# DCN-v2 cross layers on one core: input loads moved behind output transposes, an output copy two layers later, another order of the first small loads, padded biases

## The chip, the cores and the metric

The kernel runs on one core of a Trainium2 chip. Times are device microseconds of an execution; a kernel's time is the median of several. The profile is of one execution, in which a core's engines are TensorE (PE, with its weight loads as PEld), VectorE (DVE), ScalarE (ACT), GpSimd (POOL) and SyncE (SP). DMA transfers are issued by a queue of SP, of ACT or of POOL and run on 16 DMA engines that all queues share.

## What is computed

Six cross layers on a batch of 4096 rows with 416 features, all in bfloat16:

```python
# x0: (4096, 416), ws: (6, 416, 416), bs: (6, 416)
x = x0
for l in range(6):
    x = x0 * (x @ ws[l] + bs[l]) + x
return x
```

## The kernel before

**Algebra.** Every layer adds x0 times something to x. So x after layer l is x0 times (1 + the sum of all products and biases so far), and the kernel lets the matmuls of all layers add up in PSUM: a layer's output is (sum + cb[l]) * x0, where cb[l] is 1 plus the biases of layers 0 to l. These sums are made once, on PE, as a product of the biases (with a row of ones) and a triangle `u_sb` (`bias_sums`, B_BANK is bank 6), and evicted by ACT into `cb_sb`.

**Tiling.** Features lie on partitions, batch rows on the free axis. The batch is cut into four superblocks of 1024 rows (`s`, SB = 1024), each in two halves `h` of 512. The 416 features are three chunks of 128 (`c`, `m`, `k`) and a tail of 32. The tail of the four quarters of a superblock is packed onto 128 partitions (`x0t_sb`, `xt_sb`), beside a copy with neighbouring quarters exchanged ("swapped"). Six PSUM banks hold the sums of chunk m and half h, two more the tail's. Matmuls use 32-column strips of the array for the chunks, and 32-row strips for the tail inputs.

**A layer**, for each superblock: nine groups of main matmuls for half 0 (`main`), then the tail's contribution to all outputs (`tail_rows`, which needs the tail weights `wt_sb` and their corner `wc_sb`), then DVE makes half 0's next input (`leave`, L426), the tail's outputs (`tail_outs`), the tail's own eviction on ACT, its product on POOL (L449) and the swaps, split over ACT (L413) and POOL (L415), and the main matmuls and `leave` of half 1. In the last superblock's last layer, batch rows are put on partitions instead, and DVE, ACT and POOL multiply with rows of x0 (`xr_sb`) and store.

**Order of the work.** The program of each engine is written out by `Plan` in the order of the calls; every engine works through its own list in order and waits on semaphores that `Plan` derives from what is read and written. So where a call stands in the text decides what it waits behind on its engine.

**The head.** Fourteen matmuls on a constant (`fill`, L288) keep PE occupied. Superblock 0's first half is loaded as rows (`load_rows`: xin0 by SP, xin1 by ACT), transposed on PE (L497) and copied by DVE (L506); its second half, and the later superblocks, are transposed by DMA (`load_transposed`, L205, on SP). Of the tail, superblock 0's is transposed on PE from the rows and from `xtl_sb` (the tail columns of rows 512 to 1023, 128 x 4 x 32 elements), in `tail_in`, and evicted by ACT (L402). ACT's queue has, in this order: xin1, xtl, the biases `bsa_sb` (L234), and layer 0's tail weights wt0 in four pieces (L235). On PE, layer 0 goes: main k = 0, `bias_sums`, main k = 1, `tail_in`, main k = 2, `tail_rows`.

**Later superblocks.** Before, SP issues all input loads at the start: weights, then for superblocks 1, 2, 3 the transposed chunks and the last columns (`load_last_columns`, L211), then `xr_sb` (L244 to L249). `place_tail` (L219, six DMAs) puts a superblock's tail into its packed form; superblock 1's is in that list, the next ones' are issued in layer 2 of the superblock before. At a superblock's end, `transpose_block` issues four DMA transposes: three of the outputs `xo_sb` (L466) and one of the tail's `xot_sb` (L471). `store_block` (POOL's copy L477 of the tail's output, then the store L483 on SP) follows in layer 1 of the next superblock, behind that layer's tail product and swaps and ahead of the next layer's on POOL (L566, L567).

Of the kernel before, what the change touches and what calls it, by code (L numbers as in the profile page):

```python
# [118 lines left out]
def bass_standalone__dcn_v2_cross__recsys_kernel(  # L119
# [6 lines left out]
    B, D = x0.shape  # L126
    L = ws.shape[0]
# [4 lines left out]
    SB = 1024  # L132
    NS = B // SB
    H = SB // 2
    G = SB // 4
    JS = SB // 128
    NJ = B // 128
# [4 lines left out]
    with ExitStack() as es:  # L142

        def sb(name, shape, dt=BF16):
            return es.enter_context(nc.sbuf_tensor(name, shape, dt))
# [7 lines left out]
        xr_sb = sb("xr_sb", [128, JS, D])  # L153
        x0T_sb = sb("x0T_sb", [128, NC, B])
# [11 lines left out]
        ident = sb("ident", [128, 128])  # L166
        ones_sb = sb("ones_sb", [128, 128])
        dummy_sb = sb("dummy_sb", [128, 8])
        bsa_sb = sb("bsa_sb", [L + 1, D])
        u_sb = sb("u_sb", [L + 1, L])  # L170
        cb_sb = sb("cb_sb", [128, NC + 1, L], FP32)
        bt_sb = sb("bt_sb", [128, 1], FP32)
        ps = es.enter_context(nc.psum_tensor("ps", [128, 8, 512], FP32))
# [14 lines left out]
        def load(queue, dst, src, name, writes):  # L188
            P.add(queue, lambda e: e.dma_start(dst, src), writes=writes, dma=name)  # L189
# [9 lines left out]
        def load_tail_weights(a, b, name, queue="sync"):  # L199
            for q in range(4):  # L200
                load(queue, wt_sb[quad(q), a:b, :], ws[a:b, DF:D, :].rearrange("l p n -> p l n"), name, [("wt", name)])

        def load_transposed(s, a, b):
            P.add(
                "sync", lambda e: e.dma_start_transpose(x0T_sb[:, :, s * SB + a:s * SB + b], x0[s * SB + a:s * SB + b, 0:DF]),  # L205
                writes=[("x0T", s, c, h) for c in CH for h in HALVES if a <= h * H < b], dma="x0T%d" % s,
            )

        def load_last_columns(s):
            P.add(  # L210
                "sync", lambda e: e.dma_start_transpose(tT_sb[:, s - 1, :], x0[s * SB:(s + 1) * SB, D - 128:D]),  # L211
                writes=[("tT", s)], dma="tT%d" % s,
            )

        def place_tail(s):
            def part(g, o, n):
                dst, src = x0t_sb[quad(g), s, o:o + n, :], tT_sb[128 - DR:128, s - 1, (g ^ o) * G:((g ^ o) + n) * G]
                P.add(
                    "sync", lambda e: e.dma_start(dst, src.rearrange("p (o c) -> p o c", o=n)), reads=[("tT", s)],  # L219
                    writes=[("x0t", s), ("x0t", s, "swapped")], dma="x0t%d" % s,  # L220
                )

            for g in (0, 2):
                part(g, 0, 2)
            for g in (1, 3):
                part(g, 0, 1)
                part(g, 1, 1)
# [2 lines left out]
        load_rows("scalar", 1)  # L230
        for k in CH:
            load("sync", w_sb[:, 0, k, :], ws[0, 128 * k:128 * k + 128, :], "w0_%d" % k, [("w", 0, k)])
        load("scalar", xtl_sb[:, 4:JS, :], x0_v[:, 4:JS, DF:D], "xtl0", [("xtl", 0)])
        load("scalar", bsa_sb[1:L + 1, :], bs[:, :], "bs", [("bs",)])  # L234
        load_tail_weights(0, 1, "wt0", "scalar")  # L235
        load_transposed(0, H, SB)
        load_main(1)
        load_tail_weights(1, 2, "wt1")
# [2 lines left out]
        load_main(3)  # L241
        load_main(4)
        load_main(5)
        for s in range(1, NS):  # L244
            load_transposed(s, 0, SB)
            load_last_columns(s)
            if s == 1:
                place_tail(1)
        load("sync", xr_sb[:, :, :], x0_v[:, (NS - 1) * JS:NJ, :], "xr", [("xr",)])  # L249


        P.add("vector", lambda e: e.memset(ones_sb[:, :], 1.0), writes=[("ones",)])
# [7 lines left out]
                compare_op=ALU.is_equal, fill=0.0, base=0, channel_multiplier=1,  # L260
            ), reads=[("ones",)], writes=[("ident",)],
        )
        P.add("gpsimd", lambda e: e.memset(bsa_sb[0:1, :], 1.0), writes=[("bs1",)])
        P.add(
            "gpsimd", lambda e: e.affine_select(
                out=u_sb[:, :], in_=ones_sb[0:L + 1, 0:L], pattern=[[1, L]],
                compare_op=ALU.is_ge, fill=0.0, base=1, channel_multiplier=-1,
            ), reads=[("ones",)], writes=[("u",)],
        )
# [221 lines left out]
        for i in range(2):  # L491
            for c in CH:
                b = HEAD_BANKS[i][c]

                def fn(pe, i=i, c=c, b=b):
                    for j in range(2):
                        ins = pe.transpose(  # L497
                            out=psT[:, b, j * 128:(j + 1) * 128],
                            in_=xin_sb[:, 2 * i + j, c * 128:(c + 1) * 128], identity=ident[:, :],
                        )  # L500
                    return ins

                P.add("tensor", fn, reads=[("xin", i), ("ident",)], adds=[("ps", b)])
                dst, src = x0T_sb[:, c, i * 256:(i + 1) * 256], psT[:, b, 0:256]
                P.add(
                    "vector", lambda e, d=dst, s=src: e.tensor_copy(out=d, in_=s),  # L506
                    reads=[("ps", b)], writes=[("x0Tp", c, i)],
                )
        for c in CH:
            P.writer[("x0T", 0, c, 0)] = [w for i in range(2) for w in P.writer[("x0Tp", c, i)]]  # L510

        def bias_sums():
            def fn(pe):
                for c in range(NC + 1):
                    for q in range(4):
                        f0 = c * 128 + (32 * q if c < NC else 0)
                        ins = mm(
                            pe, ps[quad(q), B_BANK, c * 8:c * 8 + L], bsa_sb[:, f0:f0 + 32], u_sb[:, :],
                            c == 0, (0, 32 * q),
                        )  # L520
                return ins

            P.add("tensor", fn, reads=[("bs",), ("bs1",), ("u",)], adds=[("ps", B_BANK)])
            P.add(
                "scalar", lambda e: e.activation(
                    out=cb_sb[:, :, :],
                    in_=ps[:, B_BANK, 0:8 * (NC + 1)].rearrange("p (c e) -> p c e", e=8)[:, :, 0:L], func=ACTF.Copy,
                ), reads=[("ps", B_BANK)], writes=[("cb",)],
            )
# [3 lines left out]
        for s in range(NS):  # L533
            for l in range(L):
                ending = s == NS - 1 and l == L - 2
                if s == NS - 1 and l == L - 1:
                    break
                if s == 0 and l == 0:
                    for k in CH:
                        for part in range(2) if k == 0 else (None,):  # L540
                            for m in CH:
                                main(s, l, 0, m, k, part)
                        if k == 0:
                            bias_sums()
                        if k == 1:
                            tail_in()
                    tail_rows(s, l, True)
                    for c in CH:
                        leave(s, l, 0, c)
                    tail_outs(s, l, False)  # L550
                else:
                    for m in CH:
                        for k in CH:
                            main(s, l, 0, m, k)
                    tail_rows(s, l, l == 0)
                    for c in CH:
                        leave(s, l, 0, c)
                    tail_outs(s, l, False)
                if s == 0 and l == 1:
                    corner(2, L, "wt2")  # L560
                leave_tail(s, l, not ending)
                if l == 2 and 0 < s < NS - 1:
                    place_tail(s + 1)
                if s == 0 and l == 0:
                    corner(1, 2, "wt1")
                if l == 1 and s > 0:  # L566
                    store_block(s - 1)  # L567
                if ending:
                    P.add(
                        "gpsimd", lambda e: e.tensor_tensor(  # L570
                            out=bt_sb[:, :], in0=cb_sb[:, NC, L - 1:L], in1=cb_sb[:, NC, L - 2:L - 1], op=ALU.subtract
                        ), reads=[("cb",)], writes=[("bt",)],
                    )
                    P.add(
                        "gpsimd", lambda e, t=t32_sb[:, l % 2, :]: e.tensor_scalar_add(st_sb[:, :], t, bt_sb[:, :]),
                        reads=[("t32", l % 2), ("bt",)], writes=[("st",)],
                    )
                    for c in CH:
                        keep_sum(0, c, "scalar")
                for m in CH:  # L580
                    for k in CH:
                        main(s, l, 1, m, k)
                    leave(s, l, 1, m)
                if ending:
                    for c in CH:
                        keep_sum(1, c, ("scalar", "scalar", "vector")[c])
            if s < NS - 1:
                transpose_block(s)


        s, l = NS - 1, L - 1
# [128 lines left out]
```

## Time and profile before

| what | value |
| --- | --- |
| time, median of 3 runs | 129.0 us (128.87 to 129.28) |
| profiled execution, its own time | 130.0 us |
| its span, first to last instruction | 128.5 us |
| granted TensorE clock | 1.00 |
| L426, DVE's product into xT_sb, 120 of them | 80.9 us, 743 ns each |
| L280, PE's matmuls from xT_sb, 1596 of them | 84.2 us, 364 ns each (they overlap) |
| DMA queue of SP (q1) | 33744 packets, 13.20 MB, 48.5% of 16 engines |
| DMA queue of ACT (q10) | 1292 packets, 0.57 MB, 1.7% |

The page's busy times say which engine is nearly always at work; the chain names the work that ended last, followed back from the end; the waits say who stood still for whom, as a total, a count and the longest. In the timeline, each line has a start and a length in microseconds from the span's start, the engine (a q marks its queue of DMA issues), the line of code, the operation, and in brackets the idle time before it with what ended it. The prediction shows the lines that it rests on.

### The profile page before, as it was taken

To read this page: it belongs to the slowest core of one execution; us is meant where nothing else is said; L and a number is where in the kernel's file an instruction comes from. 1 tells how busy PE (TensorE), PEld (TensorE's weight loads), DVE (VectorE), ACT (ScalarE), POOL (GpSimd) and SP (SyncE) were. 2 spreads that over 40 slices of the span, in tenths; PEclk is the share of its full clock that TensorE was granted. 3 is DMA by queue.
4 is the path that set the end of the run, shared out by engine and by line. 5 is a ranking of instruction groups with operands and counts; after the bars stand their busy time and mean duration, and the time that the engine had idled before them with its cause. 6 is when DMAs were issued, how large, how long until landed. Compare 5 with 4: busy or idle time off the path is not lost.

```text
span 128.5 us, 5300 instructions
## 1 busy us (share of the span) xinstructions
PE 123.2 (96%) x2414; PEld 64.3 (50%) x2414; DVE 98.5 (77%) x152; ACT 43.5 (34%) x95; POOL 37.4 (29%) x79
## 2 busy tenths in 40 slices
PE   7979999999999999799999999999999999999991
PEld 5544554555545545345545545545555455455660
DVE  0329779779779779497797797797797797797973
ACT  0515225225205222343222252252222252253920
POOL 6005224134014040442221251241320351440550
PEclk9999999999999999999999999999999999999999
DMA  3998999013989894630009207200007706100017
GB/s 102 231 255 223 295 83 211 5 32 82 220 146 192 215 275 85 216 98 5 0 6 204 66 0 247 67 5 0 5 0 176 94 5 219 51 0 5 0 38 232
DMA packets 35059, 14.11 MB, mean 110 GB/s; under 512 B 25751, under 2 KB 35037, under 8 KB 35037
## 3 DMA queue, kind: packets, MB, share of 16 engines
q1 hardware_dynamic: 33744, 13.20, 48.5%
q10 hardware_dynamic: 1292, 0.57, 1.7%
q8 instruction: 19, 0.31, 1.1%
q14 instruction: 4, 0.02, 0.1%
HBM read 3.87 MB, written 3.41 MB: 57 GB/s over the span
## 4 chain that ended last, share of the span: by engine, by line
PE 83%; DMA 6%; DVE 4%; ACTq 2%; POOL 1%; issue 1%; SPq 0%
PE ps L280 83%; DMA wt_sb<-in_ws_dram 4%; DVE xT_sb L426 3%; DMA ot_sb<-xot_sb 3%; ACTq L189 2%; POOL xt_sb L415 1%; POOL xt_sb L449 0%; DVE o_sb L651 0%; SPq L466 0%; POOL o_sb L477 0%
## 5 line engine op out<-in xcount | busy, mean ns | idle before, releaser
L426 DVE SCALAR_TENSOR_TENSOR xT_sb<-ps,cb_sb,x0T_sb 128x512 bf16<-128x512 f32 x120 | 80.9, 743 | 20.2 <-PE ps L280 20.2
L280 PE MATMUL ps<-xT_sb,w_sb 128*32 128x512 bf16 (+1 forms) x1596 | 84.2, 364 | 0.0
L280 PEld LDWEIGHTS ps<-xT_sb,w_sb 128*32 128x32 bf16 x1596 | 40.9, 97 | 37.2 <-issue 4.0
L436 ACT ACTIVATE t_sb<-ps,cb_sb 64x256 f32<-64x256 f32 x46 | 21.6, 470 | 56.7 <-PE ps L280 56.4
L449 POOL TENSOR_TENSOR xt_sb<-t_sb,x0t_sb 128x256 bf16<-128x256 f32 x20 | 13.4, 672 | 59.2 <-ACT t_sb L436 59.2
L413 ACT ACTIVATE xt_sb<-xt_sb 32x256 bf16<-32x256 bf16 x38 | 15.7, 414 | 17.0 <-POOL xt_sb L449 16.7
L280 PE MATMUL ps<-x0T_sb,w_sb 128*32 128x512 bf16 (+1 forms) x348 | 18.8, 358 | 0.3 <-DVE x0T_sb L506 0.3
L415 POOL COPY xt_sb<-xt_sb 32x256 bf16<-32x256 bf16 x38 | 14.9, 393 | 2.4
L426 DVE SCALAR_TENSOR_TENSOR xo_sb<-ps,cb_sb,x0T_sb 128x512 bf16<-128x512 f32 x18 | 12.1, 742 | 2.5 <-PE ps L280 2.5
L280 PEld LDWEIGHTS ps<-x0T_sb,w_sb 128*32 128x32 bf16 x348 | 8.6, 97 | 7.8 <-issue 0.8
L280 PE MATMUL ps<-xt_sb,wt_sb 32*128 32x512 bf16 (+1 forms) x152 | 11.6, 326 | 0.8 <-POOL xt_sb L415 0.8
L280 PE MATMUL ps<-xt_sb,wc_sb 32*128 32x256 bf16 x76 | 7.3, 268 | 0.0
L280 PEld LDWEIGHTS ps<-xt_sb,wt_sb 32*128 32x128 bf16 x152 | 2.4, 91 | 8.9 <-DVE xT_sb L426 6.8
L280 PE MATMUL ps<-w_sb,xT_sb 128*32 128x416 bf16 (+1 forms) x60 | 5.1, 339 | 0.0
L449 POOL TENSOR_TENSOR xot_sb<-t_sb,x0t_sb 128x256 bf16<-128x256 f32 x3 | 2.0, 672 | 9.9 <-ACT t_sb L436 9.9
L651 DVE TENSOR_TENSOR o_sb<-ps,xr_sb 128x416 bf16<-128x416 f32 x6 | 3.4, 588 | 1.3 <-PE ps L280 1.0
L280 PEld LDWEIGHTS ps<-xt_sb,wc_sb 32*128 32x128 bf16 x76 | 3.9, 93 | 0.2
L288 PE MATMUL ps<-const-bfloat16-1.0 128*128 128x256 bf16 x14 | 3.1, 414 | 0.8 <-PEq L705 0.8
L506 DVE COPY x0T_sb<-ps 128x256 bf16<-128x256 bf16 x6 | 1.3, 282 | 3.1 <-PE ps L497 3.1
L280 PE MATMUL ps<-x0t_sb,wt_sb 32*128 32x512 bf16 (+1 forms) x32 | 2.4, 325 | 0.8 <-DMA wt_sb<-in_ws_dram 0.8
L458 ACT ACTIVATE sS_sb<-ps,cb_sb 128x512 bf16<-128x512 f32 x5 | 3.0, 691 | 0.0
L274 POOL COPY wc_sb<-wt_sb 128x32 bf16<-128x32 bf16 (+1 forms) x3 | 0.7, 237 | 7.7 <-DMA wt_sb<-in_ws_dram 7.6
(38 smaller groups left out, 26.7 us busy)
## 6 DMA issues: line engine op xcount, KB each, us to landing
out_dram<-o_sb SPq DMA_DIRECT2D x3, 832.0 KB, 4.2
w_sb<-in_ws_dram SPq DMA_DIRECT2D x5, 312.0 KB, 5.1
xr_sb<-in_x_dram SPq DMA_DIRECT2D x1, 832.0 KB, 6.4
wt_sb<-in_ws_dram SPq DMA_DIRECT2D x4, 104.0 KB, 3.5
out_dram<-o_sb SPq DMA_DIRECT2D x2, 208.0 KB, 2.2
w_sb<-in_ws_dram SPq DMA_DIRECT2D x3, 104.0 KB, 3.3
xin_sb<-in_x_dram ACTq DMA_DIRECT2D x1, 208.0 KB, 3.2
xin_sb<-in_x_dram SPq DMA_DIRECT2D x1, 208.0 KB, 3.0
```

The costliest lines, as they stand in the source:

```text
L189: P.add(queue, lambda e: e.dma_start(dst, src), writes=writes, dma=name)
L274: "gpsimd", lambda e: e.tensor_copy(out=wc_sb[:, a:b, 3 * DR:4 * DR], in_=wt_sb[:, a:b, DF:D]),
L280: return pe.matmul(dst, lhsT=lhsT, rhs=rhs, start=start, stop=True, skip_group_check=True, tile_position=pos,)
L288: ins = pe.matmul(ps[:, 7, 0:256], lhsT=const[:, 0:128], rhs=const, start=True, stop=True)
L413: fn = lambda e, d=dst, s=src: e.activation(out=d, in_=s, func=ACTF.Copy)
L415: fn = lambda e, d=dst, s=src: e.tensor_copy(out=d, in_=s)
L426: "vector", lambda e: e.scalar_tensor_tensor(out=dst, in0=ps[:, bank(h, c), :], scalar=cb_sb[:, c, l:l + 1], in1=x0T_sb[:, c, o:o + H], op ...
L436: "scalar", lambda e, p=p, h=h: e.activation(out=dst[p, :], in_=ps[p, T_BANK[h], 0:G], func=ACTF.Identity, bias=cb_sb[p, NC, l:l + 1]), re ...
L449: "gpsimd", lambda e: e.tensor_tensor(out=dst, in0=t, in1=x0t_sb[:, s, 0, :], op=ALU.mult),
L458: fn = lambda e: e.activation(out=o, in_=i, func=ACTF.Identity, bias=b)
L506: "vector", lambda e, d=dst, s=src: e.tensor_copy(out=d, in_=s),
L651: "vector", lambda e: e.tensor_tensor(out=o_sb[:, jj, :], in0=ps[:, b, 0:D], in1=xr_sb[:, j, :], op=ALU.mult), reads=[("ps", b), ("xr",)], ...
```

## The change

Four edits and a small reordering, in the text of the program:

- Superblock 1's input loads stay at the start. Those of superblock s + 2 are issued by SP behind the output transposes of superblock s, and `xr_sb` behind superblock 2's.
- `store_block` of the superblock before is called in layer 3 instead of layer 1.
- On ACT's queue the four wt0 pieces go ahead of xtl, and the biases leave that queue.
- `bsa_sb` and `u_sb` get 128 partitions in place of seven: DVE sets all of `bsa_sb` to zero and then its row 0 to one (POOL wrote that row before), and the biases are loaded by a DMA on POOL's queue, behind the zeros. `bias_sums` stands behind `tail_in` instead of ahead of layer 0's k = 1.
- DVE's six copies of transposed rows come in another order.

```diff
-        bsa_sb = sb("bsa_sb", [L + 1, D])
-        u_sb = sb("u_sb", [L + 1, L])
+        bsa_sb = sb("bsa_sb", [128, D])
+        u_sb = sb("u_sb", [128, L])
...
+        load_tail_weights(0, 1, "wt0", "scalar")
         load("scalar", xtl_sb[:, 4:JS, :], x0_v[:, 4:JS, DF:D], "xtl0", [("xtl", 0)])
-        load("scalar", bsa_sb[1:L + 1, :], bs[:, :], "bs", [("bs",)])
-        load_tail_weights(0, 1, "wt0", "scalar")
         load_transposed(0, H, SB)
...
-        for s in range(1, NS):
-            load_transposed(s, 0, SB)
-            load_last_columns(s)
-            if s == 1:
-                place_tail(1)
-        load("sync", xr_sb[:, :, :], x0_v[:, (NS - 1) * JS:NJ, :], "xr", [("xr",)])
+        load_transposed(1, 0, SB)
+        load_last_columns(1)
+        place_tail(1)
...
-        P.add("gpsimd", lambda e: e.memset(bsa_sb[0:1, :], 1.0), writes=[("bs1",)])
+        P.add("vector", lambda e: e.memset(bsa_sb[:, :], 0.0), writes=[("bs0",)])
+        P.add("vector", lambda e: e.memset(bsa_sb[0:1, :], 1.0), reads=[("bs0",)], writes=[("bs1",)])
+        P.add("gpsimd", lambda e: e.dma_start(bsa_sb[1:L + 1, :], bs[:, :]), reads=[("bs0",)], writes=[("bs",)], dma="bs")
         P.add(
             "gpsimd", lambda e: e.affine_select(
-                out=u_sb[:, :], in_=ones_sb[0:L + 1, 0:L], pattern=[[1, L]],
+                out=u_sb[:, :], in_=ones_sb[:, 0:L], pattern=[[1, L]],
...
-                dst, src = x0T_sb[:, c, i * 256:(i + 1) * 256], psT[:, b, 0:256]
-                P.add(
-                    "vector", lambda e, d=dst, s=src: e.tensor_copy(out=d, in_=s),
-                    reads=[("ps", b)], writes=[("x0Tp", c, i)],
-                )
+        for c, i in ((0, 0), (1, 0), (0, 1), (2, 0), (1, 1), (2, 1)):
+            dst, src = x0T_sb[:, c, i * 256:(i + 1) * 256], psT[:, HEAD_BANKS[i][c], 0:256]
+            P.add(
+                "vector", lambda e, d=dst, s=src: e.tensor_copy(out=d, in_=s),
+                reads=[("ps", HEAD_BANKS[i][c])], writes=[("x0Tp", c, i)],
+            )
...
-                        if k == 0:
-                            bias_sums()
                         if k == 1:
                             tail_in()
+                            bias_sums()
...
-                if l == 1 and s > 0:
+                if l == 3 and s > 0:
                     store_block(s - 1)
...
             if s < NS - 1:
                 transpose_block(s)
+            if s < NS - 2:
+                load_transposed(s + 2, 0, SB)
+                load_last_columns(s + 2)
+            if s == NS - 2:
+                load("sync", xr_sb[:, :, :], x0_v[:, (NS - 1) * JS:NJ, :], "xr", [("xr",)])
```

## The prediction

> **What bounds the kernel now.** First the page's busy times and its chain, then the waits of the whole span, then the timeline around the two waits that stop TensorE.
>
> ```profile
> PE 123.2 (96%) x2414; PEld 64.3 (50%) x2414; DVE 98.5 (77%) x152; ACT 43.5 (34%) x95; POOL 37.4 (29%) x79
> PE ps L280 83%; DMA wt_sb<-in_ws_dram 4%; DVE xT_sb L426 3%; DMA ot_sb<-xot_sb 3%; ACTq L189 2%; POOL xt_sb L415 1%; POOL xt_sb L449 0%; DVE o_sb L651 0%; SPq L466 0%; POOL o_sb L477 0%
> ...
> POOL o_sb L477 <- DMA ot_sb<-xot_sb: 4.8, 1, 4.8
> PE ps L280 <- DMA wt_sb<-in_ws_dram: 0.8, 1, 0.8
> PE ps L280 <- POOL xt_sb L415: 0.8, 1, 0.8
> ```
>
> TensorE (PE) is busy 96% of the span. It works in order, so a microsecond that it waits is a microsecond of the end unless a later wait takes it back. Two waits of 0.8 us stand out: one on the tail weights in the head, one on GpSimd (POOL) in mid-kernel. The mid one in the timeline (start, length, what):
>
> ```profile
> 41.70 6.07 SPq L466 DMA_TRANSPOSE o_sb<-xo_sb  x3
> 42.67 0.60 PE L280 MATMUL ps<-xt_sb,wt_sb 32*128 32x512 bf16 x7
> 47.55 0.60 PE L280 MATMUL ps<-xt_sb,wt_sb 32*128 32x512 bf16 x7
> 47.81 1.77 SPq L471 DMA_TRANSPOSE ot_sb<-xot_sb  x1
> 51.17 0.40 POOL L477 COPY o_sb<-ot_sb 128x256 bf16<-128x256 bf16 x1 [4.77 <-DMA ot_sb<-xot_sb]
> 53.25 0.59 PE L280 MATMUL ps<-xt_sb,wt_sb 32*128 32x512 bf16 x7 [0.76 <-POOL xt_sb L415]
> ```
>
> SyncE (SP) issues input loads until 41.7 us, so the output transposes of superblock 0 come late; POOL stands at the copy L477 until 51.17, and the tail product and swaps behind it make PE's tail rows late. Other layers take 4.88 us from tail rows to tail rows (47.55 - 42.67), this one 5.70 (53.25 - 47.55). Now the head:
>
> ```profile
> 1.30 0.53 ACTq L189 DMA_DIRECT2D xtl_sb<-in_x_dram  x1
> 1.85 0.66 ACTq L189 DMA_DIRECT2D bsa_sb<-in_bs_dram  x1
> 2.54 1.74 ACTq L189 DMA_DIRECT2D wt_sb<-in_ws_dram  x4
> 2.75 2.08 SPq L205 DMA_TRANSPOSE x0T_sb<-in_x_dram  x1
> 5.86 0.17 PEld L280 LDWEIGHTS ps<-u_sb,bsa_sb 7*32 7x32 bf16 x16 [0.21 <-issue]
> 7.16 0.60 ACT L402 ACTIVATE x0t_sb<-ps 128x512 bf16<-128x512 f32 x1 [0.77 <-PE ps L280]
> 8.52 0.59 PE L280 MATMUL ps<-x0t_sb,wt_sb 32*128 32x512 bf16 x7 [0.77 <-DMA wt_sb<-in_ws_dram]
> ```
>
> The tail rows start at 8.52 because the last of four wt0 pieces has only just landed. How long transfers on ScalarE's (ACT's) queue took, by the DMA view of narrow windows (microseconds from issue to landing at the line's end): the tail inputs, wt0's first and third piece, the input transpose, and then packets of SP's queue q1 and ACT's queue q10 from 5.05 to 5.6 us:
>
> ```profile
> xtl_sb<-in_x_dram ACTq DMA_DIRECT2D x1, 32.0 KB, 3.3
> wt_sb<-in_ws_dram ACTq DMA_DIRECT2D x1, 26.0 KB, 2.8
> wt_sb<-in_ws_dram ACTq DMA_DIRECT2D x1, 26.0 KB, 4.8
> x0T_sb<-in_x_dram SPq DMA_TRANSPOSE x1, 5.9
> q1 hardware_dynamic: 311, 0.08, 98.6%
> q10 hardware_dynamic: 1, 0.00, 0.1%
> ```
>
> What to see: while the input transpose's packets run, ACT's queue hardly moves. Pieces issued at 2.54, 2.89, 3.36 and 3.84 took 2.8, 3.8, 4.8 and 4.6 us; the last two land at 8.2 and 8.4, just before the transpose (2.75 + 5.9 = 8.6).
>
> **The change, part by part.**
>
> *Loads of superblocks 2 and 3 behind the output transposes, copy in layer 3.* Superblock 0's xo is complete at about 37.5 us, and SP, which issued later superblocks' loads from 29.5 to 41.66 before, is free to issue the transposes then. By superblock 1's rows (3.96 us for three, then 1.25) they are issued by 43 and land within 3.3 us, by 46. The copy now stands behind layer 3's swaps, about 10 us later. The 4.77 us wait goes, and PE's gap with it: 5.70 - 4.88 = **-0.82 us**. Its 0.40 us of POOL work lies in an idle gap of 3.29 us (L449's wait). What is moved later has cover: x0T of superblock 2, issued after 43, takes up to 7.0 us to issue and 9.9 to land (its tile's extremes), 53, and is wanted at 65.8. Its last columns, then the six placing DMAs (4.9 us), end by about 62 and land by 66 with the longest landing of 3.9; wanted at 67.9 by tail rows, so this has the thinnest cover, 2 us. Superblock 3 is alike one period (29.3 us) later, and xr, at about 102, has 20 us. Stores at layer 3 go out near 62, 91 and 114 us, ahead of the final ones from 124. Cost 0.
>
> *DVE copies reordered.* The first layer's third chunk writes bank 2, which the fifth copy frees in both orders: 0.
>
> *Padded biases.* Seven rows became 128. The 0.21 us PEld switch before the bias sums goes, so layer 0's second k would start at 5.76 instead of 6.05, -0.29 us where nothing later waits. The two DVE memsets (a 128x128 one took 0.17) fall in DVE's idle 3.1 us. The DMA is issued by POOL at about 1.45, replacing a 0.43 memset; no row has a POOL-issued DMA. Lower bound of its issue 0.66 (ACT's); POOL's cover is 5.3 us of idle before the corner copy. Landing: before, biases were used 4.0 us after issue, so 5.5; wanted after the tail inputs, 6.6 at the earliest. The sums' eviction now follows x0t's on ACT (0.19 us, done 0.3 us after the tail rows start; the layer's first product by cb started 0.46 after them before). Value 0; the upper bound, landing in twice that time (9.5), is what the second rival charges.
>
> *wt0 ahead of the tail inputs.* ACT issues xin1 (to 1.27), four wt0 pieces at 0.32 to 0.44, then xtl at 1.30 + 1.74 + 0.02 = 3.06 instead of 1.30. wt0 is out ahead of the transpose packets and lands near 5.5 (2.59 + 2.8): the 0.77 us wait on it goes. But xtl takes wt0's place in the shade, issued between the pieces that took 3.8 and 4.8, and with 512 packets of 64 bytes where a piece has 32. In PE's order tail_in waits for xtl, and behind it stand the bias sums, the twelve k = 2 matmuls and the tail rows. Landing X: lower bound 3.06 + 3.3 = 6.4 (its own time, no shade); upper bound about 9.0 (shade ends near 7.3, q10 needs 0.6 us for 512 packets, as it did unshaded, and the last wt0 piece landed 0.9 us after its packets). I take **X = 8.6**: a little later than wt0's last 8.4, for the larger packet count. Then tail_in at X + 0.1; from its first matmul to the end of x0t's eviction took 1.05 before (6.71 to 7.76), plus 0.1 to PE: tail rows at X + 1.25 = 9.85. PE's own work behind tail_in (0.22 + 0.13 + 0.43 + 0.32) hides in that. Against 8.52: **+1.33 us**, and the gain on the switch disappears in the same wait.
>
> The Trainium skill ("DMA: Bandwidth & Descriptors", "Queues, rings and completion order") says that a semaphore increment lands only after all earlier writes of its engine, across its queues. By it xtl cannot be reported before any transpose writes ahead of it, X near 8.6; the pieces landing at 8.2 and 8.4 agree.
>
> **Sum:** 128.5 - 0.82 + 1.33 = 129.0 us of span, 130.5 with the 1.5 us that lay around it in a profiled execution of 130.0. The same +0.5 us on the median of 129.0 gives **129.5**.
>
> **Rivals.**
>
> *The other sign: xtl gets its turns.* Mechanism: ACT's queue shares each engine with the transpose and xtl's 32 packets per engine pass before the shade is dense (256-byte packets thicken only from about 5.0; xtl could start at 4.8). For it: q10 still moved 62 packets from 4.6 to 5.05. Against: one packet in the next 0.55 us. Break-even is X + 1.25 - 8.52 = 0.82, X = 8.1. At X = 7.5 the head costs +0.23, in all -0.6: 128.4. At 6.9 or less the tail rows start by 8.15, but tail_outs needs x0T, landed 8.6, and starts at 8.72 instead of 9.07: -0.35, in all -1.2, 127.8. Middle 128.1; chance 0.32.
> The same section's rule that engines go round the queues packet by packet would make this the outcome, about 127.8 if each turn is one packet; the 1 against 311 above disagrees.
>
> *POOL's DMA is late or PE cools.* If the biases land at 9.5, bias_sums (not tail_in) sets k = 2: 9.6 + 0.13 + 0.75 = 10.5 for tail rows, +2.0, in all +1.2: 130.2. And PE starts at half speed here: the fourteen 256-column matmuls of L288 take 3.14 us, 0.22 each, as a round of 512 columns does later. If 2.2 us of waiting brought such a 3.1 us spell back, 1.6 us are lost: 131.1. The longest wait of this trace, 0.77, did not. Chance of either 0.08.
> The Trainium skill ("TensorE: Matmul & The Clock Gate", "What's actually happening") lets the clock fall only after an idle window of about 3.4 us; no run shows it yet.
>
> *The mid stall stays* (SP late again, or placing lands past 67.9): no -0.82, 130.3. Against it: 5 us and 2 us of cover. Chance 0.05.
>
> The forecast has 0.55. Its X from 8.2 to 9.0 gives +0.1 to +0.9 us, 129.1 to 129.9. About 0.3% (0.39 us) is what a measurement can tell; that is X = 8.5 and above, roughly 0.35 of the 0.55, leaving 0.20 for no change. Faster: 0.32 and a rest, 0.33; slower 0.35 + 0.12 = 0.47. The range 127.9 to 130.3 leaves out the edges of first and second rival.
>
> **What would show it.** Tail rows of layer 0 near 9.85 with PE waiting on xtl before tail_in (ACT's wait for PE instead of 0.77 grows by 2); no POOL wait on ot_sb; 4.88 us through superblock 1's layer 3; wt0's pieces landed before 6. Wrong if xtl lands by 8.0, if PE waits for bsa_sb, or if a PE gap appears near 68 or 97 us.

## The result and the profile after

The changed kernel takes 130.03 us (median of 6, 129.81 to 130.29), the one before 129.10 us in the same comparison (median of 6, 128.87 to 129.44): ratio 1.0056, 95% interval 1.0034 to 1.0077. It is slower, by 0.4 to 1.0 us.

The profiled execution of the changed kernel took 130.29 us, its span is 128.8 us. The page's chain and two of its waits, then its timeline of the head (line numbers moved: L278 is the matmul that was L280, L400 the eviction that was L402):

```profile
PE 91%; DMA 4%; ACTq 2%; DVE 0%; issue 0%
PE ps L278 91%; DMA xtl_sb<-in_x_dram 4%; ACTq L189 2%; DVE o_sb L654 0%
...
ACT x0t_sb L400 <- PE ps L278: 3.7, 1, 3.7
PE ps L278 <- DMA xtl_sb<-in_x_dram: 1.3, 1, 1.3
```

```profile
1.31 1.94 ACTq L189 DMA_DIRECT2D wt_sb<-in_ws_dram  x4
1.59 0.75 POOL L261 DMA_DIRECT2D bsa_sb<-in_bs_dram  x1 [0.16 <-issue]
2.77 1.94 SPq L205 DMA_TRANSPOSE x0T_sb<-in_x_dram  x1
3.29 0.45 ACTq L189 DMA_DIRECT2D xtl_sb<-in_x_dram  x1
8.55 0.23 PE L278 MATMUL ps<-ident,xin_sb 128*32 128x128 bf16 x2 [1.29 <-DMA xtl_sb<-in_x_dram]
9.00 0.60 ACT L400 ACTIVATE x0t_sb<-ps 128x512 bf16<-128x512 f32 x1 [3.73 <-PE ps L278]
9.65 0.60 PE L278 MATMUL ps<-x0t_sb,wt_sb 32*128 32x512 bf16 x7
```

The wait on the tail weights is gone from the chain and one on the tail inputs has come. PE stands at `tail_in` until 8.55, though the biases have landed at 6.3 and the last tail weights by 7.14 (POOL's corner copy, which waits for them, starts then), and the tail rows start at 9.65 instead of 8.52. The mid-kernel wait has gone:

```profile
37.26 3.96 SPq L464 DMA_TRANSPOSE o_sb<-xo_sb  x3
41.26 2.15 SPq L469 DMA_TRANSPOSE ot_sb<-xot_sb  x1
48.68 0.60 PE L278 MATMUL ps<-xt_sb,wt_sb 32*128 32x512 bf16 x7
53.56 0.60 PE L278 MATMUL ps<-xt_sb,wt_sb 32*128 32x512 bf16 x7
57.34 0.40 POOL L475 COPY o_sb<-ot_sb 128x256 bf16<-128x256 bf16 x1
```

The output transposes go out 4.4 us earlier, the copy stands 6 us later without a wait, and 48.68 to 53.56 is 4.88 us where it was 5.70. The two spans cut at the same places (start to layer 0's tail rows, to superblock 1's layer 3, to the last superblock's layer 4, to the end), first of after, then of before; the second number is the stretch's length:

```profile
0.00:9.65 9.65, 7.52 (x106) 4.45 (x107) 2.19 (x9) 2.14 (x4) 2.80 (x9) 1.00 0.87 199
9.65:53.56 43.91, 43.91 (x869) 22.35 (x866) 36.39 (x54) 15.09 (x35) 12.81 (x27) 1.00 0.59 109
53.56:116.98 63.42, 63.42 (x1254) 32.27 (x1250) 52.57 (x78) 21.30 (x48) 18.54 (x38) 1.00 0.39 89
116.98:128.80 11.82, 9.17 (x200) 5.66 (x196) 8.06 (x13) 4.86 (x9) 3.66 (x5) 1.00 0.45 147
```

```profile
0.00:8.52 8.52, 6.64 (x106) 4.04 (x107) 1.44 (x7) 2.28 (x4) 2.24 (x9) 1.00 0.84 185
8.52:53.25 44.73, 43.97 (x864) 22.32 (x865) 36.39 (x54) 15.07 (x34) 13.33 (x29) 1.00 0.86 160
53.25:116.67 63.42, 63.42 (x1248) 32.27 (x1249) 52.56 (x78) 21.31 (x48) 18.19 (x37) 1.00 0.28 71
116.67:128.50 11.83, 9.18 (x200) 5.67 (x196) 8.06 (x13) 4.87 (x9) 3.67 (x5) 1.00 0.23 75
```

Head +1.13, mid -0.82, the other two stretches equal: these two executions differ by 0.3 us. The medians differ by 0.93. The profiled execution of before, at 130.0 us, lies 0.9 us above its median, that of after 0.26 above its own. So part of what the profile of before shows is not in its usual execution; the experiments had to find which.

### The profile page after: what moved, and what is told of

Its sections match the earlier page's. It is cut to its first block, busy times and chain, and to the rows that moved or that the text cites. A ratio compares the mean times of both kernels' runs of the same rounds, so it can differ in the third digit from the quotient of the medians.

```text
span 128.8 us, 5303 instructions
## 1 busy us (share of the span) xinstructions
PE 124.0 (96%) x2414; PEld 64.7 (50%) x2414; DVE 99.2 (77%) x154; ACT 43.4 (34%) x95; POOL 37.8 (29%) x79
## 4 chain that ended last, share of the span: by engine, by line
PE 91%; DMA 4%; ACTq 2%; DVE 0%; issue 0%
PE ps L278 91%; DMA xtl_sb<-in_x_dram 4%; ACTq L189 2%; DVE o_sb L654 0%
## 5 line engine op out<-in xcount | busy, mean ns | idle before, releaser
L278 PE MATMUL ps<-xT_sb,w_sb 128*32 128x512 bf16 (+1 forms) x1596 | 84.2, 364 | 0.0
L278 PEld LDWEIGHTS ps<-xT_sb,w_sb 128*32 128x32 bf16 x1596 | 40.9, 97 | 37.2 <-issue 4.0
L278 PE MATMUL ps<-x0T_sb,w_sb 128*32 128x512 bf16 (+1 forms) x348 | 18.9, 363 | 0.0
L278 PEld LDWEIGHTS ps<-x0T_sb,w_sb 128*32 128x32 bf16 x348 | 8.7, 98 | 7.8 <-issue 1.0
L278 PE MATMUL ps<-xt_sb,wt_sb 32*128 32x512 bf16 (+1 forms) x152 | 11.6, 326 | 0.0
L278 PE MATMUL ps<-xt_sb,wc_sb 32*128 32x256 bf16 x76 | 7.3, 268 | 0.0
L278 PEld LDWEIGHTS ps<-xt_sb,wt_sb 32*128 32x128 bf16 x152 | 2.3, 91 | 8.1 <-DVE xT_sb L424 8.1
L278 PE MATMUL ps<-w_sb,xT_sb 128*32 128x416 bf16 (+1 forms) x60 | 5.1, 339 | 0.0
L278 PEld LDWEIGHTS ps<-xt_sb,wc_sb 32*128 32x128 bf16 x76 | 3.9, 93 | 0.3
L278 PEld LDWEIGHTS ps<-w_sb,xT_sb 128*32 128x32 bf16 (+1 forms) x60 | 2.2, 97 | 1.4 <-issue 0.2
L665 POOL TENSOR_TENSOR o_sb<-f_sb,xr_sb 128x416 bf16<-128x416 f32 x2 | 1.9, 973 | 2.9 <-ACT f_sb L661 2.9
```

Of the source, the lines that this page charges most:

```text
L278: return pe.matmul(dst, lhsT=lhsT, rhs=rhs, start=start, stop=True, skip_group_check=True, tile_position=pos,)
L665: "gpsimd", lambda e: e.tensor_tensor(out=o_sb[:, jj, :], in0=t, in1=xr_sb[:, j, :], op=ALU.mult),
```

## The experiments

Three theories were to be told apart: that the order on ACT's queue costs the time, that the padded biases or their DMA on POOL's queue do, and that the mid edit is worth less than the 0.82 us of the profile. Each ratio is to the kernel before.

**Mid-kernel edits alone (mid_only).**

```diff
 (kernel before)
-        for s in range(1, NS):
-            load_transposed(s, 0, SB)
...
+            if s < NS - 2:
+                load_transposed(s + 2, 0, SB)
...
-                if l == 1 and s > 0:
+                if l == 3 and s > 0:
```

> The kernel before with the mid-kernel edits alone: later superblocks' loads behind the output transposes and the output copy in layer 3; the head is the one of before. If the mid wait was worth what the profile of before shows, 4.88 us a layer throughout and 0.82 us less than before (ratio 0.9936). Rival: the profiled execution of before (130.0 us) is 0.9 us above the median of its runs, and its mid wait may be an exception; then the gain is 0.0 to 0.4 us (ratio 0.997 to 1.000).

Measured: 129.09 us, ratio 0.9982 (0.9959 to 1.0005). In its profile every layer takes 4.88 us, and yet the gain is about 0.2 us, and the interval includes none. What changed is the spread: its 12 executions lie between 128.63 and 129.31, while of 25 of before eight took over 129.5, up to 130.33 (a 26th, of 130.86, is not in the ratio). The mid edit takes away an upper tail more than it lowers the median.

**Order on ACT's queue put back in the changed kernel (order_back).**

```diff
 (changed kernel)
-        load_tail_weights(0, 1, "wt0", "scalar")
         load("scalar", xtl_sb[:, 4:JS, :], x0_v[:, 4:JS, DF:D], "xtl0", [("xtl", 0)])
+        load_tail_weights(0, 1, "wt0", "scalar")
```

> The changed kernel with one thing undone: on ScalarE's queue the tail inputs go ahead of the tail weights again. Theory (the tail inputs are late because they are issued into the input transpose's time): they land by 4.7 us, the tail rows of layer 0 start at 7.6 to 8.4 instead of 9.65, and the time falls 1.2 us or more below the changed kernel's, to 0.99 of the kernel before. Rival (the padded biases, their DMA on GpSimd's queue and their place behind tail_in cost the time): no fall over 0.3 us, and PE waits for the biases.

Measured: 128.80 us, ratio 0.9950 (0.9925 to 0.9975), 1.2 us below the changed kernel (1.4 by the two ratios) and better than both. Its timeline:

```profile
1.31 0.52 ACTq L189 DMA_DIRECT2D xtl_sb<-in_x_dram  x1
1.86 1.94 ACTq L189 DMA_DIRECT2D wt_sb<-in_ws_dram  x4
...
8.43 0.65 PE L278 MATMUL ps<-x0t_sb,wt_sb 32*128 32x512 bf16 x7 [0.46 <-DMA wt_sb<-in_ws_dram]
```

The tail rows start 1.2 us earlier than in the changed kernel, though they wait for the weights again. The two orders don't trade evenly: late weights hold up the tail rows alone, late tail inputs hold up `tail_in`, the bias sums, k = 2 and the eviction on ACT that the tail rows need. The ratio missed the 0.99 expected, since that took the mid edit at its full 0.82 us.

**Biases on ACT's queue, in the changed kernel (bias_act).**

```diff
 (changed kernel)
-        P.add("gpsimd", lambda e: e.dma_start(bsa_sb[1:L + 1, :], bs[:, :]), reads=[("bs0",)], writes=[("bs",)], dma="bs")
+        P.add("scalar", lambda e: e.dma_start(bsa_sb[1:L + 1, :], bs[:, :]), reads=[("bs0",)], writes=[("bs",)], dma="bs")
```

(with its memset, ahead of ACT's first activation)

> The changed kernel with the biases loaded by ScalarE's queue, behind the tail inputs, instead of GpSimd's. Theory (the order of the tail inputs is all): same as the changed kernel within 0.3 us, ratio to before 1.003 to 1.008. Rival (a DMA on GpSimd's queue costs time of its own, in the span or around it): 0.4 us or more below the changed kernel.

Measured: 130.28 us, ratio 1.0070 (1.0042 to 1.0098), as the changed kernel. POOL's queue is not what costs. In its profile xtl landed at 8.0 us and the tail rows started at 9.24, 0.4 earlier than in the changed kernel; but one layer of superblock 0 (tail rows at 19.00 and 24.21) took 5.21 us instead of 4.88, and why is open.

**Order on ACT's queue alone (swap_only).**

```diff
 (kernel before)
+        load_tail_weights(0, 1, "wt0", "scalar")
         load("scalar", xtl_sb[:, 4:JS, :], x0_v[:, 4:JS, DF:D], "xtl0", [("xtl", 0)])
         load("scalar", bsa_sb[1:L + 1, :], bs[:, :], "bs", [("bs",)])
-        load_tail_weights(0, 1, "wt0", "scalar")
```

> The kernel before with the tail weights ahead of the tail inputs on ScalarE's queue, then the biases; nothing else. Theory: tail inputs land near 8.4 us and the tail rows of layer 0 start near 9.7 instead of 8.5, 1.1 to 1.3 us slower than before (ratio 1.009 to 1.010), with the biases waited for as well since they now come last but are wanted ahead of k = 1. Rival (order does not matter, tail weights and tail inputs trade places): within 0.3 us of before.

Measured: ratio 1.0193 (1.0142 to 1.0244), twice the loss expected; the median of all six executions is 132.04 us, that of the five in the ratio 131.79. The expectation had the biases' wait in words but not in its sum:

```profile
8.51 0.26 PE L280 MATMUL ps<-u_sb,bsa_sb 7*32 7x6 bf16 x16 [2.73 <-DMA bsa_sb<-in_bs_dram]
...
10.46 0.60 PE L280 MATMUL ps<-x0t_sb,wt_sb 32*128 32x512 bf16 x7
```

PE stands 2.73 us ahead of k = 1 with everything else behind it; the tail rows start at 10.46, 1.94 later than before. Moving `bias_sums` behind `tail_in` is what keeps the changed kernel from this: bias_act, which has the biases last on ACT's queue as here but sums them behind `tail_in`, does not wait for them. The two executions at a mean granted clock of 1.000, the profiled one among them, took 131.13 and 131.17 us, 1.9 above before, as the tail rows have it. The other four took 131.79 to 134.10 at mean granted clocks of 0.974 to 0.987, where all executions of the other kernels but b_delay (below) have 0.997 to 1.000. The profile also runs the mid-kernel code of before without its wait: SP issued the output transposes from 38.06 there, 3.6 us ahead of the first profile of before.

**The kernel before, profiled again (b_again).** No edit.

> The kernel before once more, for a second profile of it. If the mid wait of its first profile was an exception of a late SyncE list, this one has a span near 127.7 us, 4.88 us through superblock 1's layers, and no wait of GpSimd on ot_sb above 1 us. Rival (the wait is in nearly every execution): 5.7 us in layer 2 of superblock 1 again and a span of 128.3 or more.

Measured: 129.73 us, a span of 128.2, and the wait again:

```profile
POOL o_sb L477 <- DMA ot_sb<-xot_sb: 4.8, 1, 4.8
...
PE ps L280 <- POOL xt_sb L415: 0.8, 1, 0.8
```

The expectation that it would be gone failed, and the execution is again 0.5 us above the median of before beside it (129.18). Both executions of before that were profiled lie in its upper part, and both have the wait.

**One more input load in SP's list (b_delay).**

```diff
 (kernel before)
+        spare_sb = sb("spare_sb", [128, NC, SB])
...
                 place_tail(1)
+                P.add("sync", lambda e: e.dma_start_transpose(spare_sb[:, :, :], x0[SB:2 * SB, 0:DF]),
+                      writes=[("spare",)], dma="spare")
```

> The kernel before with one more transposed load of 1024 rows, into a tile that nothing reads, in SyncE's list behind superblock 1's loads: some 4 us of list time added. Theory (the mid wait comes when SyncE's list of input loads runs late): GpSimd waits for ot_sb in the profile, one layer takes 5.5 us or more, and the median is 0.6 to 3 us above before (ratio 1.005 to 1.023). Rival (the list's length does not matter): same as before.

```profile
POOL o_sb L482 <- DMA ot_sb<-xot_sb: 5.4, 1, 5.4
...
PE ps L285 <- POOL xt_sb L420: 1.4, 1, 1.4
```

Measured: ratio 1.0068 (1.0026 to 1.0110), from three executions of 130.1 to 130.2 us; five others had a granted clock of 0.975 to 0.987 and took 133 to 136 us, and with no profile of one, why is open. In the profiled one POOL's wait is 5.42 us and the layer takes 6.36, 1.48 over the usual. Before it was 4.77 and 0.82. Wait less loss is 3.95 and 3.94 us: so much of POOL's wait at the copy is covered by its idle time, and every microsecond beyond goes to PE. So the loss follows from how late SP comes to the output transposes: at 42.44 us here, at 41.70 and 41.48 in the two profiles of before. The added load's 4.04 us of issue made that only 0.7 us later, since earlier entries of the list went faster in this execution (the placing DMAs from 21.80 instead of 24.73).

**The biases alone (pad_only)** (changed kernel with the order put back and the mid-kernel of before).

```diff
 (kernel before)
-        load("scalar", bsa_sb[1:L + 1, :], bs[:, :], "bs", [("bs",)])
...
+        P.add("gpsimd", lambda e: e.dma_start(bsa_sb[1:L + 1, :], bs[:, :]), reads=[("bs0",)], writes=[("bs",)], dma="bs")
...
-                        if k == 0:
-                            bias_sums()
                         if k == 1:
                             tail_in()
+                            bias_sums()
```

> The kernel before with the padded biases alone: 128 partitions, loaded by GpSimd's queue, summed behind tail_in (and the reordered copies); order of the tail inputs and mid-kernel as before. Theory (this edit gains because the tail weights are issued 0.7 us earlier on ScalarE's queue): 0.2 to 0.5 us below before, ratio 0.996 to 0.9985. Rival (nothing but order and mid edits move the time): 0.9985 to 1.001.

```profile
POOL o_sb L478 <- DMA ot_sb<-xot_sb: 3.5, 1, 3.5
```

Measured: 128.87 us, ratio 0.9980 (0.9949 to 1.0010): the gain expected lies inside the interval, and so does none. In its profile SP comes to the output transposes at 39.16, POOL waits 3.5 us at the copy, below the 3.95, and the layer of the copy takes 4.88: the same mid-kernel code as before, without loss. Its tail rows start at 8.08. Three of its 12 executions took 129.6 to 130.3 us, the upper tail that before has and mid_only and order_back, with the new mid-kernel, have not (129.31 and 129.14 at most).

**The input transpose issued later, in the changed kernel (shade_late).**

```diff
 (changed kernel)
-        load_transposed(0, H, SB)
         load_main(1)
         load_tail_weights(1, 2, "wt1")
+        load_transposed(0, H, SB)
```

> The changed kernel with the input transpose of superblock 0's second half issued 2.4 us later by SyncE, behind layer 1's weights. Theory (the transpose's packets hold up ScalarE's queue): the tail inputs, issued at 3.3 us as in the changed kernel, land by 7 us instead of 8.4 (3.3 to 3.7 us after issue instead of 5.1), and PE waits for x0T in tail_outs instead. Rival (the queue is full anyway, with whatever lies on SyncE's): they land at 8 us or later.

The DMA view's line for xtl, of the changed kernel and then of this one:

```profile
xtl_sb<-in_x_dram ACTq DMA_DIRECT2D x1, 32.0 KB, 5.1
```

```profile
xtl_sb<-in_x_dram ACTq DMA_DIRECT2D x1, 32.0 KB, 4.3
```

Measured (one execution): 129.53 us, xtl landed at 7.6. Between theory and rival: without the transpose beside it xtl is 0.8 us faster, but not as fast as when it goes first (3.4 in order_back). The transpose is part of its lateness, about half; what the rest is was not tried. x0T itself landed 3.9 us after its issue instead of 5.9, and PE did not wait for it.

**Two tail weight pieces on POOL's queue, order put back (split_wt0, split_again; order_back again is order_again).**

```diff
 (order_back)
-        load_tail_weights(0, 1, "wt0", "scalar")
+        for q in (0, 1): load("scalar", ...)
...
+        for q in (2, 3): load("gpsimd", ...)
```

> order_back with two of the four tail weight pieces on GpSimd's queue, ahead of the biases, so that all are issued before the input transpose's packets run. Theory: the pieces land by 6.5 us, tail rows start at 7.6 to 8.0, tail_outs then waits for x0T (8.6), and the time is 0.2 to 0.4 us below order_back's (ratio to before 0.992). Rival (GpSimd's queue is as late as ScalarE's, or pieces on it take longer): same as order_back, 0.995.

> split_wt0 once more, beside order_back on the same chip. If the tail rows' 0.6 us earlier start in its profile is worth what it shows: 0.3 us or more below order_back. Rival (x0T's landing or other waits take it back in most executions): within 0.15 us of order_back.

> order_back once more, on the same chip as split_again: ratio to before 0.993 to 0.997 as in its first run.

Measured: 128.66 us and, again, 128.83 us, ratios 0.9961 (0.9935 to 0.9986) and 0.9956 (0.9935 to 0.9977); order_back again 128.82 us, 0.9958 (0.9942 to 0.9975). In the profile no tail weight is waited for and the tail rows start at 7.83, 0.6 us ahead of order_back's first profile:

```profile
1.44 1.26 POOL L189 DMA_DIRECT2D wt_sb<-in_ws_dram  x2
1.86 1.00 ACTq L189 DMA_DIRECT2D wt_sb<-in_ws_dram  x2
...
7.83 0.60 PE L281 MATMUL ps<-x0t_sb,wt_sb 32*128 32x512 bf16 x7
```

The medians show none of it, as the rival had it. order_back's second profile explains some: there the weights cost 0.22 us and the tail rows started at 7.93. So how late the weights are varies by execution too, and the simpler order_back is as good.

**PE kept at work in swap_only's wait (swap_fill).**

```diff
 (swap_only)
                         if k == 0:
+                            fill(24)
                             bias_sums()
```

> swap_only with 24 more matmuls on the constant (2.6 us of PE time, results unused) in PE's list ahead of the bias sums, where swap_only's PE stands for 2.7 us. Theory (swap_only's executions of 131.8 us and more, at a mean clock of 0.987, lost the clock in that wait: 0.013 x 131 = 1.7 us): every execution has clock 0.995 or more and takes 130.8 to 131.4 us, a median 0.7 us or more below swap_only's 132.0. Rival (the slow ones come from elsewhere): median within 0.3 us of 132.0 and clocks of 0.987 again.

```profile
6.11 2.87 PE L288 MATMUL ps<-const-bfloat16-1.0 128*128 128x256 bf16 x24
```

Measured: 131.77 us, ratio 1.0184 (1.0146 to 1.0221). All four executions (131.41 to 131.98) have a mean granted clock of 1.000, but they miss the 130.8 to 131.4 us expected, and their median is that of swap_only's five (131.79). Against swap_only's two at full clock (131.15) they lose 0.6 us; 0.4 of it is that the added matmuls run on after the biases were there in swap_only (the sums start at 8.90 instead of 8.51). That the clock stayed up in four of four against two of six fits the theory; with so few executions it is not proof, and in the time nothing was gained.

## Why the prediction was right, and where its sum was off

**The head, the step that decided it.** The forecast was that xtl, issued at 3.06 in wt0's old place, would land at 8.6, and that tail_in and the work in order behind it would put the tail rows at 9.85: +1.33 us. The trace has 3.29, 8.41 and 9.65: +1.13. order_back, which undoes this one step, is 1.2 us faster than the changed kernel (130.03 to 128.80, and 128.82 the second time), 1.4 by the ratios, so the step is shown and its size was right. That it agrees to 0.2 us is partly luck, since the head varies by execution: four profiles with the head of before have their tail rows at 8.16 to 8.65. One part of this step was off and cost nothing: the last wt0 piece was to land near 5.5 and landed by 7.14, still ahead of xtl.

**Why xtl is late** was only half right. The prediction took it that ACT's queue hardly moves beside the transpose. In the changed kernel it does move, here from 5.6 to 7.6 us and then from 7.65 to 8.4 (queue: packets, MB, share):

```profile
q1 hardware_dynamic: 1217, 0.34, 95.5%
q10 hardware_dynamic: 519, 0.03, 20.4%
...
q1 hardware_dynamic: 232, 0.19, 109.3%
```

Nearly all of xtl's 512 packets pass in the first stretch, in turns with the transpose's; in the second q10 has none left, and still xtl is not reported until 8.41. So ACT's queue does get its turns, as the rival said, though not ahead of the transpose's dense packets, as it needed, but among them. What the transpose adds can be read from shade_late, where q10 has no packet left from 6.7 to 7.55 while SP's queue, the transpose's packets nearly all, goes on:

```profile
q1 hardware_dynamic: 701, 0.18, 99.7%
```

There xtl is reported at 7.6, 1.5 us ahead of the transpose (5.17 + 3.9 = 9.07), some 0.9 us behind its last packet; in the changed kernel that delay is 0.8. So the 0.8 us that shade_late recovers of the 1.7 (3.4 to 5.1) lie in when the packets pass, and not in the report. The Trainium skill's rule that the prediction cited ("DMA: Bandwidth & Descriptors", "Queues, rings and completion order": a semaphore increment lands only behind all earlier writes of its engine, from any queue) may lie behind this delay. That the report waits for the transpose is not shown, since the delay is as long where the transpose is reported much later. The forecast's 8.6 was the landing of wt0's last piece, 8.4, carried over to a transfer in the same place. That comparison was good; with the reason given for it, a queue that hardly moves, the figure is partly luck.

**The mid edit** was taken at -0.82 us. In the profiled pair that is exact (44.73 to 43.91). In the comparisons it is worth 0.2 us (mid_only, 0.9982, with an interval that reaches 1.0005). This is the term that was mis-sized: the sum was made against one execution and its difference carried over to a median that the execution lies 0.9 us above. The wait at the copy has 3.95 us of cover (before, b_delay), pad_only's 3.5 us cost nothing, and so the edit gains only in executions in which SP's list is late. How many those are is not shown; eight of 25 executions of before lie above 129.5 us. It is also why the time came out 0.5 us above the 129.5 forecast. And it bore on the sign: with the mid edit at its full 0.82 us, bias_act's xtl at 8.0, below the sum's break-even of 8.1, would have meant no loss, and bias_act measured 1.0070.

**The biases** were taken at 0 in the sum. Their two possible harms, a late POOL transfer and its cost on POOL, did not come: issued in 0.75 us, landed 4.7 us later at 6.3 (5.5 was assumed), wanted at 8.7; bias_act, at 1.0070 against 1.0056, shows no cost of POOL's queue. A gain that the order hides in the changed kernel shows in order_back: it and mid_only differ by the biases' edit (with the reordered copies) alone, 128.80 against 129.09 in the same comparison. pad_only's interval can't confirm it. Where the biases leave ACT's queue, the weights are issued 0.68 us earlier (1.86 instead of 2.54); that this is the cause was not tried by itself.

Put together, by ratios: mid -0.2%, biases -0.3%, order +1.1%, in all +0.6%. The first two are differences about as large as their intervals.

**The covers** held: superblock 2's loads and placing (issued until 55.5 us) and superblock 3's cause no wait; all layers behind the head take 4.88 us. **PE cooling**, a rival at small chance, did not come in the changed kernel (1.3 us of wait, clock 1.00); lower clocks came in swap_only, with a wait of 2.7.

## What to carry to other kernels

Before two transfers trade places, ask for each what stands behind its consumer on an in-order engine: late weights held one step, late inputs held four. A small transfer whose packets pass among those of a long one on another queue comes late (5.1 us for xtl instead of 3.4, half of it for the long one), so what is wanted first goes out before it. And before a wait in a profile is priced, set that execution's own time against the median: 0.9 us of difference was larger than the wait itself.

## What was not expected of the hardware

- A wait of PE of 2.7 us may cost it clock. swap_only shows mean clocks of 0.987 in three executions of 131.8 to 132.4 us and 1.000 in two of 131.1 to 131.2. By the clock 0.013 x 131 = 1.7 us were lost, by the times 0.6 to 1.3. With PE kept busy through the wait, four of four kept 1.000. The Trainium skill ("TensorE: Matmul & The Clock Gate", "What's actually happening") names half rate after an idle window of about 3.4 us, and full rate after a busy one as long; 3.4 us of work at half rate would lose 1.7 us, an estimate from its figures that agrees with the mean clock. The profiled wait of 2.73 us kept the clock, and those that lost it were not profiled, so the length that suffices is open. That the wait is the cause is not proved either: b_delay, with the head of before, has five executions at 0.975 to 0.987.
- PE's first matmuls take different times in equal code. The twelve transposes behind the fourteen equal matmuls, in before (most of them 219 ns) and in after (most of them 314 ns):

```profile
3.81 0.89 PE L497 MATMUL ps<-ident,xin_sb 128*128 128x128 bf16 x12
```

```profile
3.95 1.46 PE L495 MATMUL ps<-ident,xin_sb 128*128 128x128 bf16 x12
```

  mid_only has 1.46, order_back 0.84, and the granted clock of this stretch (3.80 to 5.45) reads 1.00 in all four, so what sets it is open. In the changed kernel this 0.6 us is hidden by the wait for xtl.
- A transpose of the same rows takes 3.9 us to land when issued 2.4 us later (5.17) and 5.9 beside the head's other loads (shade_late, after).
